# Position bias as a product of two exact factors, and a second expert's first 384 rows beside the attention stage

## The chip, the cores and the metric

The kernel runs on one core of a Trainium2 chip. The metric is device time in microseconds (us). The kernel before took 684.06, 686.87 and 689.18 us in three runs, 686.87 in the median. PE is the matmul engine (PEld its weight loads), DVE, ACT and POOL are the vector, scalar and GpSimd engines, and SP is the engine whose queue issues most of the DMAs. Every engine takes its instructions in the order in which they were emitted.

## What is computed

Eight batches and eight heads of causal attention with a window of 128 and a linear position bias, then a top-1 mixture of eight experts on the 4608 resulting rows of 512:

```python
scores = scale * np.matmul(q, k.transpose(0, 1, 3, 2))      # 8, 8, 576, 576; D = 64
bias = slopes[:, None, None] * (-np.abs(rel))               # rel = query - key
mask = (rel >= 0) & (rel < 128)
attn = softmax(np.where(mask, scores + bias, -1e9))
x = (attn @ v) as rows of 512
expert_idx = argmax(xn @ en.T / tau); gate_w = its softmax value
out[mask_e] = gate_w * (relu(x @ w1[e]) @ w2[e])            # w1 512x1024, w2 1024x512
```

With the inputs used, the experts get 611, 541, 517, 513, 507, 670, 573 and 676 rows; among the first 24 of 36 tiles expert 5 has 479 and expert 7 has 453. The kernel has eight slots with room for 672, 688, 624, 576, 544, 528, 528 and 512 rows (`SLOTS`, L34), and a loop for rows beyond them (L1586) that runs no iteration here.

## The kernel before

**Attention.** The 576 rows of a batch are cut into four tiles of 128 and a rest of 64; the rests of two batches make one "pair" tile. That gives 36 tiles: per two batches two "first" ones (no tile before them in the window), six "full" ones and one pair. A tile is worked in two units of four heads, 72 units in all. A unit is: scores (`score_pe`, L552) into two PSUM banks; for full and pair tiles a merge of the two key blocks by a mask (`merge_dve`), a maximum (`max_dve`), an exponential (`exp_act`), a transpose (`probs_pe`, "flip"), a split into a high and a low half in fp16 (`probs_act`, `probs_dve`), masks on POOL, and the product with v (`values_pe`). `score_pe` first puts the bias into the two banks: an identity matrix (128 rows) is multiplied with a table of the bias in bf16 (L564), which has 512 columns for each bank of a full tile, 256 and 128 in two matmuls for a pair and 256 for a first tile. The q and k products then add to it, as pairs of matmuls on rows 0 to 63 and 64 to 127 of the array. The tables are built at the start (`bias_table`, L268: two "wrap" operations and eight products on DVE for each of two kinds; `first_table`).

**Routing.** Each finished tile is split (`x_act`, `x_pool`), transposed by a DMA (`x_dma`, L738) and gives its logits. Six groups of tiles (`GROUPS`, L39: 8, 8, 8, 6, 4 and 2) are routed together: a chain of small DVE and ACT operations, a matmul for ranks (`ranks`, L790), and scatters of the rows into an array sorted by expert (`put`, L847). The buffers of the split rows (`gx`) are 13 in a ring and come free with the scatters.

**The head.** After the third group (24 tiles) the expert with most rows so far is chosen (`head_ops`, L295). SP reads its number, fetches its weights in 16 pieces of 256 KB (`fetch`, L891) into six staging buffers, ACT and DVE split them (`part_hi`, `part_lo`), its first 384 rows are loaded by a transposing DMA (`head_rows`, L904), and both its matmul layers for them are done in pieces of four matmuls (`head_hidden`, `head_output`) that fill PE between the attention units.

**The expert stage.** `moe` (L1220) then goes through the slots in the order `TURNS` (L35), 0 first and then 1. Slot 0 is the head's expert, from row 384 on; the others take all their rows. `blank_rows` and `rows` (L1258) load a slot's rows, which needs every scatter done; `fetch` and `part` bring and split its weights, by turns into pools `wE`, `wO` and `wT`; `hidden` (L1348) and `output` (L1393) are its matmuls.

**Order.** A planner (`Plan`, L69) writes the order of each engine by hand: every piece of work is a job with an engine, an assumed duration, what it comes after, ring buffers it takes, and a due time. Of the jobs that can start within a slack of the earliest one of an engine it takes those not marked `fill` first, then the one due first. A dependency with `ORDER` fixes only the order of picking. One plan covers attention, routing and head, a second one the expert stage; the whole first plan stands ahead of the second in each queue.

## Time and profile before

| | |
|---|---|
| runs, median (lowest to highest) | 686.87 us (684.06 to 689.18) |
| profiled execution | 687.89 us, of which the span is 686.2 us |
| granted PE clock over the span | 0.974 of full speed |
| busy share PE, PEld, DVE, ACT, POOL | 94, 62, 55, 49, 38% |
| DMA traffic | 109.83 MB, 160 GB/s over the span |

The shares are means over two stages: attention with routing and head up to about 306 us, the experts from 320 us on. A group of instructions is named by its line, engine, operation and tiles (written <- read), and each row gives the start, or the busy time and the mean duration of one. "Idle" is the time in which the engine stood still before an instruction, with what released it.

### The profile page before, as it was taken

What the parts mean: (1) busy time and instruction counts of PE and PEld (TensorE: products, weight loads), DVE (VectorE), ACT (ScalarE), POOL (GpSimd) and SP (SyncE); (2) the same over time, 40 slices, a digit from 0 to 9 for tenths busy, and PEclk for the clock granted to TensorE, in tenths of its full rate; (3) what the DMA queues carried; (4) which work ended last, traced back from release to release, by engine and by line L of the source; (5) the groups of instructions that cost most, each with busy time, mean ns of one, the idle gap of its engine ahead of it and who ended that gap; (6) DMA issues with size and microseconds to landing.
All of it is one profiled execution on the core that took longest, in us unless ns stands there. A gap on an engine that the chain in (4) does not pass through costs nothing. (4 is left out here: it accounts for less than half of the span.)

```text
span 686.2 us, 15721 instructions
## 1 busy us (share of the span) xinstructions
PE 644.3 (94%) x6059; PEld 427.9 (62%) x6059; DVE 380.3 (55%) x985; ACT 332.8 (49%) x777; POOL 257.4 (38%) x427
## 2 busy tenths in 40 slices
PE   8999999998998899883999999999999999999993
PEld 5778767776785667542666476476584764754442
DVE  6888878785896997560336724344244265210250
ACT  5988868885886876410325524333243244210210
POOL 5757578658768635851020110120111112001011
PEclk9999999998999999995999999999999999999998
DMA  9789989896987896247999963924919555001000
GB/s 194 149 146 187 149 229 168 153 194 183 185 171 232 170 217 155 78 116 173 269 234 373 222 260 64 287 99 89 312 48 254 189 101 201 17 16 47 13 31 31
DMA packets 217676, 109.83 MB, mean 160 GB/s; under 512 B 195829, under 2 KB 195829, under 8 KB 217600
## 3 DMA queue, kind: packets, MB, share of 16 engines
q1 hardware_dynamic: 211760, 89.89, 58.1%
q0 software_dynamic: 5840, 18.92, 7.4%
q8 instruction: 48, 0.79, 0.5%
q14 instruction: 28, 0.23, 0.1%
HBM read 61.92 MB, written 28.12 MB: 131 GB/s over the span
## 5 line engine op out<-in xcount | busy, mean ns | idle before, releaser
L1354 PE MATMUL ps<-xT,w1h 128*128 128x272 f16 (+7 forms) x896 | 176.1, 296 | 14.3 <-DMA xT<-xs 13.7
L1354 PE MATMUL ps<-xT,w1l 128*128 128x272 f16 (+7 forms) x448 | 132.7, 296 | 0.0
L1354 PEld LDWEIGHTS <-w1h 128*128 128x128 f16 x896 | 88.4, 99 | 46.1 <-issue 15.2
L365 POOL DMA_INDIRECT out_dram<-y,ids x32 | 35.2, 1099 | 206.0 <-DVE y L1412 107.0
L1362 DVE SCALAR_TENSOR_TENSOR hl<-ps,hh 128x272 f16<-128x272 f32 (+7 forms) x112 | 51.6, 474 | 107.3 <-ACT hh L1364 101.0
L1364 ACT ACTIVATE hh<-ps 128x272 f16<-128x272 f32 (+7 forms) x112 | 45.7, 424 | 115.5 <-PE ps L1354 114.5
L1398 PE MATMUL ps<-w2h,hh 128*128 128x512 f16 (+1 forms) x264 | 98.4, 373 | 0.0
L1398 PE MATMUL ps<-w2l,hh 128*128 128x512 f16 (+1 forms) x264 | 98.4, 373 | 0.0
L1398 PE MATMUL ps<-w2h,hl 128*128 128x512 f16 (+1 forms) x264 | 98.4, 373 | 0.0
L609 ACT ACTIVATE pe<-sc,nm 128x128 f32<-128x128 f32 x288 | 84.6, 378 | 10.9 <-DVE nm L602 8.6
L1398 PEld LDWEIGHTS <-hh 128*128 128x128 f16 x528 | 51.5, 98 | 58.6 <-issue 0.8
L585 PE MATMUL sc<-kh,qh 64*128 64x128 f32 (+2 forms) x768 | 75.5, 343 | 0.5 <-ACT qh L462 0.5
L585 PEld LDWEIGHTS sc<-kh,qh 64*128 64x128 f32 (+1 forms) x768 | 51.4, 182 | 28.3 <-issue 23.9
L462 ACT ACTIVATE pq<-ptp 128x512 f16<-128x512 f32 x72 | 54.2, 753 | 22.0 <-PE ptp L617 14.6
L465 DVE SCALAR_TENSOR_TENSOR pq<-ptp,pq 128x512 f16<-128x512 f32 x72 | 52.8, 733 | 21.0 <-ACT pq L462 18.0
L602 DVE TENSOR_REDUCE nm<-sc 128x2 f32<-128x256 f32 x144 | 55.9, 410 | 4.1 <-PE sc L585 3.6
L617 PE MATMUL ptp<-ident,pe 128*128 128x128 f32 x288 | 48.4, 287 | 10.4 <-ACT pe L609 3.5
L734 POOL TENSOR_TENSOR gx<-xf,gx 128x512 f16<-128x512 f32 x36 | 42.5, 1181 | 30.7 <-DVE gx L723 22.2
L1329 DVE SCALAR_TENSOR_TENSOR w2l<-ws,w2h 128x1024 f16<-128x1024 f32 x28 | 33.9, 1223 | 35.6 <-ACT w2h L1331 33.3
L1354 PEld LDWEIGHTS <-w1l 128*128 128x128 f16 x448 | 44.3, 99 | 15.0
L1329 DVE SCALAR_TENSOR_TENSOR w1l<-ws,w1h 128x1024 f16<-128x1024 f32 x28 | 33.4, 1223 | 35.0 <-ACT w1h L1331 34.9
L1331 ACT ACTIVATE w2h<-ws 128x1024 f16<-128x1024 f32 x28 | 29.1, 1054 | 42.5 <-DMA ws<-moe_w_dram 40.3
(227 smaller groups left out, 1187.5 us busy)
## 6 DMA issues: line engine op xcount, KB each, us to landing
ws<-moe_w_dram SPq DMA_DIRECT2D x56, 512.0 KB
ldk<-k_dram SPq DMA_DIRECT2D x32, 256.0 KB
ldq<-q_dram SPq DMA_DIRECT2D x32, 256.0 KB
ldv<-v_dram SPq DMA_DIRECT2D x32, 256.0 KB
stg<-moe_w_dram SPq DMA_DIRECT2D x16, 256.0 KB
xs<-zrow SPq DMA_DIRECT2D x3, 1092.2 KB
xs<-zrow SPq DMA_DIRECT2D x1, 1413.5 KB
xs<-zrow SPq DMA_DIRECT2D x1, 1285.0 KB
```

What stands on the lines that cost most here:

```text
L462: nc.scalar.activation(hi, ps, AF.Copy, scale=scale)
L465: nc.vector.scalar_tensor_tensor(lo, ps, scale, hi, op0=ALU.mult, op1=ALU.subtract)
L585: nc.tensor.matmul(sc[T, hf, j][o, l, w], qT[T]["h"][rows, hp, o], at["h"][rows, hp, kc], start=False, stop=True, skip_group_check=True,)
L602: nc.vector.tensor_reduce(nm_t[T, hf, j], sc[T, hf, j][:, :, 0:P], axis=AX.X, op=ALU.min)
L609: nc.scalar.activation(pr_t[T, hf][:, 2 * l + j, :], ps[:, l, 0:P], AF.Exp, bias=nm[:, l : l + 1], scale=-1.0)
L617: nc.tensor.transpose(pt[:, i, :], pe[:, i, :], ident)
L734: nc.gpsimd.tensor_tensor(xx[:, DM : 2 * DM], xf_t[T], xx[:, 0:DM], op=ALU.subtract)
L1329: nc.vector.scalar_tensor_tensor(lo_, x, SW, hi, op0=ALU.mult, op1=ALU.subtract)
L1354: nc.tensor.matmul(ps[:, :w], a[:, kt, fs], xx[:, b + kt, c0 : c0 + w], start=(n == 0), stop=(n == len(jobs) - 1))
L1362: nc.vector.scalar_tensor_tensor(hl[:, ft, c0 : c0 + w], ps[:, :w], 0.0, hi, op0=ALU.max, op1=ALU.subtract)
L1364: nc.scalar.activation(hi, ps[:, :w], AF.Relu)
L1398: nc.tensor.matmul(ps, x[:, ft, a * P : (a + 1) * P], w[:, ft, c], start=(n == 0), stop=(n == len(jobs) - 1))
```

## The change

Bias: the bias of query c and key column t is slope x (c + 128 - t) for the tile before and slope x (c - t) for the tile's own keys, that is two products: a column factor (c, 1) and a row factor (slope, slope x (128 - t)). The two factors stand in two rows, padded with zeros to 64, once at partition 0 and once at partition 64; for full and pair tiles one matmul of 64 rows for each of the two banks takes the place of the identity matmuls of 128 rows. The tables for "full" and "pair" go, and `bias_factors` builds the factors.

Second expert: after the third group the expert with the second most rows is chosen too (`second_ops`). Its weights are fetched once the last tile's loads are issued, into 11 `gx` buffers and five staging buffers, and split into the buffers of k, q and v loads and of the transposed k, which are moved to a pool of their own (`rot`) that stays for the expert stage and takes the place of `wO`. Its first 384 rows go through both layers in pieces marked `fill`, behind the head's. Slot 1 then starts at its row 384 with weights that are there. The planner's durations for scores fall, and on DVE and ACT a late, urgent job that can start within 400 ns goes ahead of a fill job.

```diff
+HB = HEAD
+IN_STG = [7, 8, 9, 14, 15]
+GAP = {"DVE": 400, "ACT": 400}
+URGENT = 190000
...
+                if f and e in GAP:
+                    soon = [(t_, j["name"]) for t_, j in lst if not j["fill"] and j["due"] >= URGENT and t_ <= t0 + GAP[e]]
+                    if soon:
+                        t, n = min(soon)
...
+    def bias_factors():
+
+        col = const.tile([P, 2, P], F32, tag="wrap", name="wrap_cols")
+        nc.gpsimd.memset(bcol, 0.0)
+        nc.gpsimd.memset(brow, 0.0)
+        nc.gpsimd.iota(col, pattern=[[-P, 2], [-1, P]], base=P, channel_multiplier=0, allow_small_or_imprecise_dtypes=True)
+        for j in range(2):
+            two, one = slice(64 * j, 64 * j + 2), slice(64 * j, 64 * j + 1)
+            nc.gpsimd.memset(bcol[two], 1.0)
+            nc.gpsimd.iota(bcol[one, 0, :], pattern=[[1, P]], base=0, channel_multiplier=0, allow_small_or_imprecise_dtypes=True)
...
+            for hf in range(2):
+                for l in range(2):
+                    x, sl = brow[:, hf, l], slopes[4 * hf + 2 * l + j]
+                    nc.vector.tensor_scalar(x[two], col[two], sl, None, op0=ALU.mult)
+                    nc.vector.memset(x[one], sl)
...
+            ("DVE", 90, lambda: V.tensor_scalar(k1("r1"), k1("n1"), float(HB), None, op0=ALU.min)),
+            ("DVE", 90, lambda: V.tensor_copy(k1("r1i", I32), k1("r1"))),
+            ("SP", 1500, lambda: head_box["second"]()),
...
-                tab = tabs[kind][:, 4 * hf + j : 4 * hf + j + 3 : 2, :]
-                if kind == "full":
-                    biases = [(ps.rearrange("p l (a c) -> p l a c", a=2), tab.unsqueeze(2).to_broadcast([P, 2, 2, P]))]
-                elif kind == "pair":
-                    biases = [(ps[:, :, 0:P], tab), (ps[:, :, P : P + REM], tab[:, :, 0:REM])]
+                rows = slice(64 * j, 64 * j + 64)
+                if kind == "first":
+                    o, a_, b_ = ps[:, :, 0:P], identb, tabs[kind][:, 4 * hf + j : 4 * hf + j + 3 : 2, :]
                 else:
-                    biases = [(ps[:, :, 0:P], tab)]
-                for n, (o, b_) in enumerate(biases):
-                    nc.tensor.matmul(o, identb, b_, start=(n == 0), stop=False, skip_group_check=True)
+                    w = P + REM if kind == "pair" else 2 * P
+                    o, a_ = ps[:, :, 0:w], bcol[rows, int(kind == "pair"), :]
+                    b_ = brow[rows, hf].rearrange("p l a c -> p l (a c)")[:, :, 0:w]
+                nc.tensor.matmul(o, a_, b_, start=True, stop=False, skip_group_check=True)
...
+        def second_start():
+            sd["e"] = nc.sync.value_load(sel_["se"][0:1, 0:1], min_val=0, max_val=E - 1)
+            sd["r"] = nc.sync.value_load(sel_["r1i"][0:1, 0:1], min_val=0, max_val=HB)
...
+        def second_rows():
+            sd["x"] = xa.tile([P, 2 * KT, HEAD], F16, tag="x_head", name="x_second")
...
-                    f"score{u}", "PE", 660 if first else 1000 if pair else 1300, lambda a=a: score_pe(*a),
+                    f"score{u}", "PE", 660 if first else 850 if pair else 1100, lambda a=a: score_pe(*a),
...
+                f"fetch2_{i}", "SP", 800, lambda i=i: second_fetch(i),
+                after=[second] + ldz + [(f"fetch{x}", ORDER) for x in range(NP)] + [(f"xhi{TL - 2 if i < 10 else TL}", ORDER), (f"xdma{TL if i > 9 else TL - 3}", ORDER)] + ([(f"y{a}", ORDER) for a in range(HEAD // P)] if i in IN_STG[3:] else []) + ([(f"fetch2_{i - 1}", ORDER)] if i else []),
+                makes=[("stg" if i in IN_STG else "gx", ("stg2", i))], due=d,
...
+                made = [(f"k{b}h", ("w1b", b, x)) for b in range(2) for x in range(2)]
...
+            J(f"wlo2_{i}", "DVE", 602, lambda i=i: second_lo(i), after=[f"whi2_{i}"], uses=[("stg2", i)], due=d + 5500, fill=True)
+        J(
+            "rows2", "SP", 3000, second_rows, after=[second, f"hid{FT - 1}_2", (f"xdma{TL}", ORDER)] + ldz + seen, due=due("load", 2 * NT),
+        )
...
+                dep = ["rows2", (f"out{HEAD // P - 1}_5", ORDER)] + [f"wlo2_{w0 + i}" for i in range(KT)] if c == 0 else [f"hid2_{ft}_{c - 1}"]
...
+                dep = [f"hlo2_{ft}" for ft in range(FT)] + [f"wlo2_{2 * KT + i}" for i in range(FT)] if c == 0 else [f"out2_{a}_{c - 1}"]
...
         def first_row(s):
-            return HEAD if s == 0 else 0
+            return {0: HEAD, 1: HB}.get(s, 0)
...
-            if p:
+            if p > 1:
```

The functions of the second expert that are left out (`second_fetch`, `second_hi`, `second_lo`, `second_hidden`, `second_hhi`, `second_hlo`, `second_output`, `second_y`, `second_put`) do what those of the head do, with the same instruction shapes.

## Rows read from the trace of the kernel before

**Rows 1.** One row of the page: the mean clock granted to PE, in tenths, in 40 equal slices of the span.

```profile
PEclk9999999998999999995999999999999999999998
```

**Rows 2.** Busy time by stretches of the span (from:to, length, then PE, PEld, DVE, ACT and POOL busy with the count of instructions, granted clock, DMA share, GB/s), first of the attention stage, then around its end.

```profile
20.00:40.00 20.00, 19.99 (x292) 16.00 (x290) 16.58 (x53) 18.29 (x51) 13.63 (x21) 1.00 0.72 141
60.00:80.00 20.00, 20.00 (x299) 15.70 (x297) 15.52 (x51) 16.82 (x47) 12.28 (x20) 1.00 0.94 148
200.00:220.00 20.00, 16.80 (x220) 12.40 (x216) 13.99 (x54) 12.46 (x36) 15.14 (x26) 1.00 0.78 219
280.00:300.00 20.00, 20.00 (x255) 12.52 (x255) 12.72 (x50) 6.89 (x20) 11.70 (x19) 0.96 0.32 66
306.00:320.00 14.00, 0.41 (x2) 0.00 (x0) 3.40 (x21) 0.00 (x0) 5.06 (x10) 0.60 0.68 181
320.00:326.00 6.00, 5.94 (x26) 3.83 (x27) 0.46 (x1) 0.41 (x1) 0.78 (x4) 0.51 0.73 146
```

**Rows 3.** What PE waited for, longest in total first (total, times, longest one).

```profile
PE ps L1354 <- DMA xT<-xs: 13.7, 1, 13.7
...
PE ptp L617 <- issue: 2.9, 1, 2.9
```

**Rows 4.** PE in order of time at the end of the first plan and the start of slot 0 (start, length, line, operation, count, idle before it).

```profile
305.23 0.17 PE L790 MATMUL ptr<-oh,tri 128*128 128x16 bf16 x1
306.03 0.38 PE L952 MATMUL ps_head<-w2h,hl_head 128*128 128x512 f16 x1
320.06 0.64 PE L1354 MATMUL ps<-xT,w1h 128*128 128x288 f16 x2 [13.66 <-DMA xT<-xs]
```

**Rows 5.** The scatters on POOL and the DMA issues of SP that lead from the last attention tile to slot 0, in order of time, and the head's row load.

```profile
279.26 18.78 SPq L738 DMA_TRANSPOSE xT<-gx  x4
296.80 1.23 SPq L738 DMA_TRANSPOSE xT<-gx  x1
301.00 0.99 POOL L847 DMA_INDIRECT xs<-gx,di  x1 [0.99 <-DVE di L834]
311.00 0.97 POOL L847 DMA_INDIRECT xs<-gx,di  x1 [0.28 <-POOL gx L846]
315.48 2.38 SPq L1265 DMA_TRANSPOSE xT<-xs  x1
L907 SPq DMA_TRANSPOSE x_head<-xs x1: 4275/4275/4275, 225.1 to 225.1; - x1
```

**Rows 6.** Scores on PE, in order of time: of a full unit (bias, q and k product, and the next unit's flip), of a first unit (bias, product) and of a pair unit (bias, product).

```profile
25.25 0.59 PE L564 MATMUL sc<-tab_full,identb 128*128 128x512 bf16 x2
25.77 1.13 PE L585 MATMUL sc<-kh,qh 64*128 64x256 f32 x8
26.84 0.66 PE L617 MATMUL ptp<-ident,pe 128*128 128x128 f32 x4
31.13 0.38 PE L564 MATMUL sc<-tab_first,identb 128*128 128x256 bf16 x2
31.44 0.71 PE L585 MATMUL sc<-kh,qh 64*128 64x128 f32 x8
124.73 0.49 PE L564 MATMUL sc<-tab_pair,identb 128*128 128x256 bf16 x4
125.16 0.88 PE L585 MATMUL sc<-kh,qh 64*64 64x192 f32 x16
```

**Rows 7.** The q and k products of full units as one group up to 300 us, shapes kept apart (count, busy us, mean ns of one).

```profile
L585 PE MATMUL sc<-kh,qh 64*128 64x256 f32 x256 | 37.0, 408 | 0.0
```

**Rows 8.** The head's split of its hidden layer on DVE and ACT, as groups (count, busy us, mean ns of one), and its weights' fetches and DVE halves by line (min/median/max ns, first and last start).

```profile
L935 DVE SCALAR_TENSOR_TENSOR hl_head<-ps_head,hh_head 128x384 f16<-128x384 f32 x8 | 4.4, 551 | 2.7 <-ACT hh_head L931 2.6
L931 ACT ACTIVATE hh_head<-ps_head 128x384 f16<-128x384 f32 x8 | 3.9, 492 | 4.6 <-PE ps_head L928 4.5
L893 SPq MOVE stg<-moe_w_dram x16: 13/29/687, 209.1 to 246.3; - x16
L900 DVE SCALAR_TENSOR_TENSOR w1l<-stg,w1h x8: 653/1258/1653, 221.6 to 241.8; 128x512 f16<-128x512 f32 x8
L900 DVE SCALAR_TENSOR_TENSOR w2l<-stg,w2h x8: 673/682/685, 243.6 to 256.2; 128x512 f16<-128x512 f32 x8
```

**Rows 9.** The head's pieces on PE, in order of time: two matmuls of 384 columns with two more between them, then two of 512 columns, one right after the other.

```profile
273.05 0.33 PE L928 MATMUL ps_head<-x_head,w1l 128*128 128x384 f16 x1
...
273.53 0.33 PE L928 MATMUL ps_head<-x_head,w1l 128*128 128x384 f16 x1
...
303.50 0.38 PE L952 MATMUL ps_head<-w2h,hh_head 128*128 128x512 f16 x1
303.72 0.38 PE L952 MATMUL ps_head<-w2l,hh_head 128*128 128x512 f16 x1
```

**Rows 10.** The start: DVE and POOL work for tables, and the first unit's maximum, in order of time.

```profile
8.15 0.76 DVE L602 TENSOR_REDUCE nm<-sc 128x2 f32<-128x256 f32 x2 [2.02 <-PE sc L585]
9.42 1.84 POOL L995 MEMSET tails<- 128x1024 f16 x2
11.77 1.98 DVE L277 TENSOR_SCALAR tab_pair<-wrap_pair 128x128 bf16<-128x128 f32 x8
```

**Rows 11.** The choice of the head on DVE, first and last of its eight operations.

```profile
205.56 0.15 DVE L305 COPY hc<-ptr 128x8 f32<-128x8 f32 x1
207.96 0.14 DVE L312 CAST he<-hf 128x1 int32<-128x1 f32 x1
```

More of the change, by code (lines that the diff above doesn't have):

```diff
@@ new lines, in second_hidden @@
+        def second_hidden(ft, c):
+            if ft == 0 and c == 0:
+                sd["h"] = [hp_.tile([P, FT, HEAD], F16, tag=f"h{n}_head", name=f"h{n}_second") for n in "hl"]
+            if c == 0:
+                sd["ps1", ft] = bank("sc", [P, 512], name=f"ps1_second_{ft}")[:, :HB]
+            w, ps = head_box["w1b"], sd["ps1", ft]
+            jobs = [(a, b, kt) for kt in range(KT) for a, b in ((0, 0), (0, KT), (1, 0))]
+            for n in range(4 * c, 4 * c + 4):
+                a, b, kt = jobs[n]
+                nc.tensor.matmul(
+                    ps, w(a, kt)[:, ft * P : (ft + 1) * P], sd["x"][:, b + kt, :], start=(n == 0), stop=(n == len(jobs) - 1)
+                )
@@ new lines, in second_hhi, with second_hlo, second_output @@
+        def second_hhi(ft):
+            nc.scalar.activation(sd["h"][0][:, ft, :], sd["ps1", ft], AF.Relu)
+        def second_hlo(ft):
+            hh, hl = sd["h"]
+            nc.vector.scalar_tensor_tensor(hl[:, ft, :], sd["ps1", ft], 0.0, hh[:, ft, :], op0=ALU.max, op1=ALU.subtract)
+        def second_output(a, c):
+            if c == 0:
+                sd["ps2", a] = bank("sc", [P, DM], name=f"ps2_second_{a}")
+            w = head_box["w2b"]
+            jobs = [(x, v_, ft) for ft in range(FT) for x, v_ in ((0, 0), (0, 1), (1, 0))]
+            for n in range(4 * c, 4 * c + 4):
+                x, v_, ft = jobs[n]
+                nc.tensor.matmul(
+                    sd["ps2", a], sd["h"][x][:, ft, a * P : (a + 1) * P], w(v_, ft), start=(n == 0), stop=(n == len(jobs) - 1)
+                )
@@ new lines, in attention @@
+        J(
+            "rows2", "SP", 3000, second_rows, after=[second, f"hid{FT - 1}_2", (f"xdma{TL}", ORDER)] + ldz + seen, due=due("load", 2 * NT),
+        )
+        J("info2", "DVE", 400, second_info, after=["rows2", "order11"], due=1e7)
+        for ft in range(FT):
+            w0 = 0 if ft < FT // 2 else KT
+            for c in range(3):
+                dep = ["rows2", (f"out{HEAD // P - 1}_5", ORDER)] + [f"wlo2_{w0 + i}" for i in range(KT)] if c == 0 else [f"hid2_{ft}_{c - 1}"]
+                J(
+                    f"hid2_{ft}_{c}", "PE", 4 * 162, lambda a=(ft, c): second_hidden(*a), after=dep + ([f"hid2_{ft - 1}_2"] if ft and c == 0 else []),
+                    makes=[(RING["sc"], ("ps1b", ft))] if c == 0 else [], uses=[("ps1b", ft)], due=3e7 + 1000 * ft, fill=True,
+                )
+            J(f"hhi2_{ft}", "ACT", 370, lambda ft=ft: second_hhi(ft), after=[f"hid2_{ft}_2"], uses=[("ps1b", ft)], due=0)
+            J(f"hlo2_{ft}", "DVE", 470, lambda ft=ft: second_hlo(ft), after=[f"hhi2_{ft}"], uses=[("ps1b", ft)], due=0)
@@ new lines, in attention @@
+        for a in range(HB // P):
+            for c in range(6):
+                dep = [f"hlo2_{ft}" for ft in range(FT)] + [f"wlo2_{2 * KT + i}" for i in range(FT)] if c == 0 else [f"out2_{a}_{c - 1}"]
+                J(
+                    f"out2_{a}_{c}", "PE", 4 * 216, lambda b=(a, c): second_output(*b), after=dep + ([f"out2_{a - 1}_5"] if a and c == 0 else []),
+                    makes=[(RING["sc"], ("ps2b", a))] if c == 0 else [], uses=[("ps2b", a)], due=4e7 + 1000 * a, fill=True,
+                )
+            J(
+                f"y2_{a}", "ACT" if a % 2 else "DVE", 600, lambda a=a: second_y(a),
+                after=[f"out2_{a}_5", "info2"] + [f"fetch2_{i}" for i in IN_STG], makes=[("stg", ("y2", a))], uses=[("ps2b", a)], due=2e7,
+            )
+            J(f"yput2_{a}", "POOL", 1200, lambda a=a: second_put(a), after=[f"y2_{a}"], uses=[("y2", a)], due=3e7)
@@ L1376, in passes @@
         def passes(h, w):
[L1377 removed]
+            return [(x, w(v_, ft), ft) for ft in range(FT) for x, v_ in ((h[0], 0), (h[0], 1), (h[1], 0))]
         ps2 = {}
@@ L1481, in moe @@
                         f"hid{n}", 12 * (0.407 * w_ + 5.5), lambda a=a: hidden(*a),
-                        [f"rows{s}"] + ([f"wlo1_{s}_{c}" for c in range(4)] if p else []),
+                        [f"rows{s}"] + ([f"wlo1_{s}_{c}" for c in range(4)] if p > 1 else []),
                         makes=[("pt", ("ps1", n))], uses=[("xT", s), ("w", 1, s)], due=t0,
```

234 lines of the change are left out of this document (180 added, 54 removed).

## Prediction

> **What bounds the kernel now.** I read the clock by slices first: PE runs at full clock but for one slice at half, past the middle [rows 1]. The busy times by stretches say where: in 306 to 320 us PE works 0.41 us of 14, and in 320 to 326 it works with a granted clock of 0.51, the lower level of 1.2 GHz [rows 2]. The list of waits names the largest one of PE, 13.7 us once, until slot 0's rows are loaded [rows 3], and the order of time shows both ends: the head's last piece at 306.03 plus 0.38, slot 0's first matmul at 320.06 [rows 4]. It is a chain of latencies: last x transpose issued at 296.80, last scatter at 311.00, row load at 315.48, first matmul 4.6 us later [rows 5]. Outside it PE is the bound: in 20 to 40 and 60 to 80 it is busy 39.99 us of 40; ACT is next with 18.29 of 20, and the DMA share is 0.94 in the later of the two [rows 2]. From 320 us on no wait of PE is among the long ones [rows 3], so what is taken from PE's work there comes off the end.
>
> **The moved matmuls.** Slot 1 had 688 rows in two chunks, now 384 early and 304 late: the hidden layer has the same 2 x 96 matmuls with the same sum of columns, and 3 + 2 row blocks replace five. PE's work thus neither falls nor rises; it moves from the expert stage to before slot 0. It is 96 matmuls at a pitch of 0.48 / 3 = 0.16 us, 15.4 us, and 72 at 0.216 (303.72 less 303.50, with rounding), 15.5 us [rows 9]: 30.9 us. That is more than the gap, so if the operands are ready it closes the gap wholly: **-13.65 us** of idle time, and the slow clock behind it, 320.06 to about 325.8 at half pace, **-2.9 us** [rows 2, 4]. Slot 0 then starts at about 306.4 + 30.9 + waits, near 340, while its rows are there at 320: the chain has some 19 us of slack, so DVE's 16 weight halves, the puts of the second's rows and everything else that stretches the routing is covered by second-expert matmuls up to that point.
>
> **When its operands come.** Its rows: the transposing load stands on SP right behind the last x transpose, whose issue ends at 298.03. The head's same load took 4.28 us to issue [rows 5]; slot 0's began to be used 2.2 us after its issue ended (320.06 less 317.86), so the rows are there at about 304.5, before the head's last piece. Its w1: tile buffers come free with the last scores (282); fetches go out behind the transpose at 279.26 [rows 5]. At the head's own pace, 209.1 to 242.4 for w1 and to 256.9 for all 16 [rows 8], w1 would be split at 313, when the fifth of eight hidden blocks wants it at 314, and w2 at 327, when the output wants it at 323.5. That pace was DVE's while it was nearly full; in 280 to 300 it is busy 12.72 us of 20 and ACT 6.89 [rows 2]. Late operands: 0 to 5 us, I take **+2**, nearer the lower end because both engines have room. Between the layers PE waits for the last block's halves, 0.49 on ACT and 0.55 on DVE [rows 8] with two handoffs: **+1.5**.
>
> **Transfers in front of transposes.** Ten of the 16 fetches (2.6 MB) may go out between the last four x transposes. PE takes its queue in order and stands at a logit until its transpose has landed. The nearest row is 219.80, where PE stood 2.9 us for nothing that the trace shows, while the head's fetches were in flight [rows 3]. Three transposes behind fetches: 0 to 8.7 us, I take **+3**, one such stop, because the last transposes are up to 5 us apart. Fetches 10 to 13 wait for the buffers of tiles 30 to 33, whose scatters begin at 301.00 [rows 5]; behind them on SP stand only the blanking and rows of slot 0, which have the slack above.
>
> **The choice of the second.** Twelve more DVE operations and two reads on SP. The head's eight took 205.56 to 208.10, 0.32 each [rows 11], so 3.8 us more before SP can go on; queued behind it are fetches, loads and transposes. PE is busy only 16.80 of 20 us there [rows 2]. 0 to 3 us, I take **+1**.
>
> **The bias.** A full unit's bias takes 25.25 to 25.77, 0.52 us, for two matmuls of 512 columns (2 x 0.216, and 0.09 until the next weights are in); a first unit's, half the columns, takes 0.31, a pair's 0.43 [rows 6]. That two 64-row matmuls run side by side the trace shows: eight q and k products of 408 ns each [rows 7] take 1.07 us from their start to the flip [rows 6], while at the pitch of 0.216 of a matmul of about this length (0.38, [rows 9]) they would take 1.73. So a full unit falls to about 0.31, as the first unit with the same columns in a row: 48 x 0.21 = 10.1 us; a pair unit from 768 columns in a row to 384: 8 x 0.16 = 1.3 us. Of 11.4 us PE time the first 200 us give most, where PE is full, but the next bounds are near (ACT 91% and DMA 0.94 [rows 2]), and where PE waits for others nothing is gained. Bounds 0 and -11.4; I take **-8**, nearer the upper end since the packed stretches hold most units.
>
> The Trainium skill, TensorEngine Tiling (Array Packing), Key Properties, speaks against a part of it: a change of tiling mode drains the engine. In full units the change only moves from behind the bias to before it; in pair units (64 x 128, then 64 x 64) one is added. No row here shows such a drain by itself; by the rule the pair units' gain would be near nothing and the sum about 1 us higher.
>
> **The start.** On DVE the four wrap operations and the pair table (1.98 us, [rows 10]) go; eight products and eight small memsets come, some 3 us, but ahead of the first unit's maximum (8.15) and behind about 2.6 us of POOL work, of which one memset of 128 x 1024 is half of 1.84 [rows 10]. The first units come up to 2.7 us later, and what the pair table delayed comes earlier. -1 to +3, I take **+1**.
>
> **Sum.** 687.89 (this execution) - 13.65 - 2.9 - 8 + 2 + 1.5 + 3 + 1 + 1 = 671.8. The execution is 1.0 us above the median of the runs; for the median that is **671 us**.
>
> **Rivals.** *The bias pays nothing*: the two matmuls run one after the other, or ACT and DMA set the pace. For it: ACT's 18.29 of 20; against: PE's 39.99 of 40 and the pairs of q and k products. 671 + 8 = 679. *The operands come late*: the matmuls stand where I put them, but PE waits 11 us for them instead of 2, w2 above all, since six of its eight fetches stand behind the last transpose and the scatters. Then 671 + 9 = 680. *Slower, the gap moves*: if the second's pieces stand in PE's queue before the last group's rank matmul (305.23, [rows 4]), the chain from there to slot 0, 14.8 us, begins only when they are done, and its idle time and slow clock stand behind them instead of before. Nothing is won at the end, the waits of 8.5 us remain: 687.89 - 1 + 8.5 - 8 = 687 with the bias's gain, 695 without. It decides from about 19 us of delay of that matmul on. For it: both stand in one fixed order made with assumed durations; against: fill pieces yield to any job that is ready, and these need a load behind the last transpose.
>
> **Chances.** Forecast 0.62 (664 to 678), bias nothing 0.13, late operands 0.14, gap moves 0.06, better than 664 0.05 (at best 661: -11.4 for the bias and no wait but 1.5 and the start). About 1% (680 and 694 us) is what a measurement of this kernel can tell from no change. Faster: 0.62 + 0.05, half of each of the two cases at the border, which spread some us around 679 and 680, less a little for waits that add up: 0.78. Same: the rest of these and most of the moved gap, 0.16. Slower: 0.06, the moved gap without the bias's gain, or several waits at their upper ends. The range reaches from the best case's neighbourhood to late operands at their worst, 660 to 683.
>
> **What would show it.** The bias: between its first matmul and the first q and k product 0.3 us in place of 0.52, and the two bias matmuls starting together; the last scores come some 8 us earlier. The gap: PE's wait for slot 0's rows gone, no slice at half clock, slot 0 starting 12 to 20 us after 320 less what attention gained, at full clock. The waits: idle of PE before second-layer pieces under 3 us. I am wrong if PE stands more than 10 us in all before the second's matmuls, if units keep their spacing (3 us and more) with a shorter bias, or if later expert slots wait for weights.

## The result and the profile after

The changed kernel takes 692.22 us (median of 6 runs, 690.17 to 693.65) against 687.19 of the kernel before: 1.0073 times, 95% interval 1.0049 to 1.0097. I had said 671 us. Its profiled execution took 691.89 us with a span of 689.8.

The clock by slices (as [rows 1]) and busy time by stretches (as [rows 2]):

```profile
PEclk9999999999998999997999999999999999999998
```

```profile
20.00:40.00 20.00, 19.80 (x287) 16.78 (x289) 17.76 (x55) 18.50 (x52) 14.20 (x20) 1.00 0.69 133
280.00:300.00 20.00, 18.50 (x235) 11.34 (x228) 12.22 (x38) 8.98 (x25) 12.88 (x19) 0.91 0.76 199
300.00:320.00 20.00, 8.77 (x81) 4.48 (x79) 12.46 (x40) 5.01 (x14) 11.35 (x17) 0.81 0.51 134
320.00:326.00 6.00, 6.00 (x35) 3.29 (x34) 3.50 (x21) 3.70 (x7) 0.57 (x2) 0.78 0.92 280
360.00:380.00 20.00, 16.24 (x88) 8.76 (x86) 10.84 (x17) 8.30 (x14) 0.97 (x1) 0.91 0.81 209
```

There still is a hole, with a lower clock in it and behind it: PE works 8.77 us of 20 in 300 to 320. And there is a second, small one in 360 to 380, where before was nearly full. Before, in the same stretch:

```profile
360.00:380.00 20.00, 19.33 (x121) 11.62 (x119) 13.01 (x17) 11.93 (x19) 0.00 (x0) 1.00 1.09 351
```

What PE waited for (as [rows 3]):

```profile
PE ptl L813 <- DMA xT<-gx: 14.0, 6, 8.6
...
PE ps L1644 <- DVE hl L1608: 3.8, 1, 3.8
PE ps_second L1117 <- DMA x_second<-xs: 2.6, 1, 2.6
```

The wait for slot 0's rows is gone, as intended. In its place PE waits for the x transpose of the last attention tile, for the second expert's rows, and inside slot 0. PE in order of time (as [rows 4] and [rows 6]): the bias and the product of a full unit, the last two scores (with one matmul of the head's output layer ahead of the last), the last logit, the second's first piece, the last rank matmul, slot 0's hidden and output layer.

```profile
269.20 0.39 PE L633 MATMUL sc<-brow,bcol 64*128 64x512 bf16 x2
269.42 0.39 PE L654 MATMUL sc<-kh,qh 64*128 64x128 f32 x4
...
279.17 0.34 PE L633 MATMUL sc<-brow,bcol 64*128 64x384 bf16 x2
...
290.45 0.38 PE L1021 MATMUL ps_head<-w2l,hh_head 128*128 128x512 f16 x1
290.76 0.34 PE L633 MATMUL sc<-brow,bcol 64*128 64x384 bf16 x2
...
316.87 0.28 PE L813 MATMUL ptl<-enc,xT 128*128 128x16 f16 x4 [8.61 <-DMA xT<-gx]
...
319.87 2.72 PE L1117 MATMUL ps_second<-x_second,w 128*128 128x384 f16 x8 [2.63 <-DMA x_second<-xs]
322.39 0.22 PE L859 MATMUL ptr<-oh,tri 128*128 128x16 bf16 x1
...
353.48 0.42 PE L1600 MATMUL ps<-xT,w1h 128*128 128x288 f16 x2 [0.85 <-DVE y_second L1144]
...
369.17 0.38 PE L1644 MATMUL ps<-w2h,hh 128*128 128x512 f16 x1 [3.76 <-DVE hl L1608]
```

Read from the end: the last logit waits for a transpose whose issue comes at 312.41 instead of 296.80 [rows 5]. POOL and SP, in order of time:

```profile
300.86 0.88 POOL L719 TENSOR_SCALAR_AFFINE_SELECT tails<-pq 64x256 f32<-64x256 f32 x2 [7.69 <-DVE cd L894]
...
304.90 0.97 POOL L916 DMA_INDIRECT xs<-gx,di  x1 [0.28 <-POOL gx L915]
...
310.07 1.12 POOL L916 DMA_INDIRECT xs<-gx,di  x1 [0.28 <-POOL gx L915]
311.22 1.16 POOL L803 TENSOR_TENSOR gx<-xf,gx 128x512 f16<-128x512 f32 x1
```

```profile
312.41 1.23 SPq L807 DMA_TRANSPOSE xT<-gx  x1
313.83 3.95 SPq L1084 DMA_TRANSPOSE x_second<-xs  x1
```

The last unit's mask begins at 300.86, so its rows are late; the lower half of the last x (311.22) then stands on POOL behind the four scatters of the group before. And the unit is late from its score on: 290.76 against 280.64 in before:

```profile
280.64 0.85 PE L564 MATMUL sc<-tab_pair,identb 128*128 128x256 bf16 x4
```

Between the last two scores PE does, beside the flips and the products with v of other units, much of the head's output layer (two of its three products in the 11.8 us from 279, by operand):

```profile
L1021 PE MATMUL ps_head<-w2h,hh_head x9: 378/379/381, 278.6 to 290.2; 128*128 128x512 f16 x9
L1021 PE MATMUL ps_head<-w2l,hh_head x9: 379/379/379, 278.9 to 290.5; 128*128 128x512 f16 x9
```

In before no output piece stands ahead of the last score (the first one starts at 283.55); here eight do, of four matmuls each, six of them between the last two scores. The planner wrote it so: a score takes two of the four banks of the ring `sc`, an output block one, and a bank is handed on in turn. With the shorter durations that the change gives scores (1100 and 850 ns), block 0 is planned just ahead of the last score but one, and the last score's second tile then falls to block 0's bank and cannot be planned until the block is finished; block 1 fills the time.

Slot 0's own wait is ACT's order. ACT, then SP:

```profile
365.22 1.06 ACT L1577 ACTIVATE w2h<-ws 128x1024 f16<-128x1024 f32 x1 [17.05 <-DMA ws<-moe_w_dram]
366.44 1.06 ACT L1577 ACTIVATE w2h<-ws 128x1024 f16<-128x1024 f32 x1 [0.16 <-DMA ws<-moe_w_dram]
367.40 2.50 ACT L1610 ACTIVATE hh<-ps 128x288 f16<-128x288 f32 x8
```

```profile
348.35 6.43 SPq L1550 DMA_DIRECT2D ws<-moe_w_dram  x4
354.97 1.38 SPq L1552 DMA_DIRECT2D ws<-moe_w_dram  x2
```

ACT stands 17.05 us at slot 4's weight halves, whose loads SP issues from 348.35 on; the eight halves of slot 0's hidden layer stand behind and then run without a wait, in 2.50 us.

### The profile page after: what moved, and what is told of

Read it like the earlier page. It is cut to its first block, busy times and chain, and to the rows that moved or that the text cites. A ratio compares the mean times of both kernels' runs of the same rounds, so it can differ in the third digit from the quotient of the medians.

```text
span 689.8 us, 15768 instructions
## 1 busy us (share of the span) xinstructions
PE 634.5 (92%) x6043; PEld 425.4 (62%) x6043; DVE 384.6 (56%) x1015; ACT 334.1 (48%) x785; POOL 257.8 (37%) x440
## 4 chain that ended last, share of the span: by engine, by line
PE 71%; DMA 8%; DVE 7%; POOL 5%; ACT 4%; issue 3%; SPq 1%; POOLq 0%; ACTq 0%
PE ps L1644 22%; PE ps L1600 21%; PE sc L654 5%; PE av L754 5%; DMA xT<-gx 4%; PE ptp L686 4%; PE ps_second L1117 2%; PE ptk L543 2%; PE sc L633 2%; PE ps_t L1634 2%; DMA ws<-moe_w_dram 2%; PE ps_second L1135 2%; POOL xs L916 1%; PE ptq L543 1%; ACT pq L532 1%
## 5 line engine op out<-in xcount | busy, mean ns | idle before, releaser
L1608 DVE SCALAR_TENSOR_TENSOR hl<-ps,hh 128x272 f16<-128x272 f32 (+5 forms) x104 | 47.1, 469 | 97.6 <-ACT hh L1610 90.0
L1600 PE MATMUL ps<-xT,w1h 128*128 128x272 f16 (+4 forms) x448 | 81.2, 284 | 0.8 <-DVE y_second L1144 0.8
L1600 PE MATMUL ps<-xT,w 128*128 128x288 f16 (+4 forms) x576 | 78.9, 299 | 0.0
L1600 PEld LDWEIGHTS <-w 128*128 128x128 f16 x576 | 56.4, 98 | 22.4
L1600 PE MATMUL ps<-xT,w1l 128*128 128x272 f16 (+4 forms) x224 | 63.6, 284 | 0.0
L1644 PE MATMUL ps<-w2h,hh 128*128 128x512 f16 x152 | 58.3, 384 | 3.8 <-DVE hl L1608 3.8
L1644 PE MATMUL ps<-w2l,hh 128*128 128x512 f16 x152 | 58.4, 384 | 0.0
L1644 PE MATMUL ps<-w2h,hl 128*128 128x512 f16 x152 | 58.2, 383 | 0.0
L1600 PEld LDWEIGHTS <-w1h 128*128 128x128 f16 x448 | 43.8, 98 | 12.1 <-DVE y_second L1144 1.3
L1644 PE MATMUL ps<-w,hh 128*128 128x512 f16 (+1 forms) x176 | 48.1, 360 | 0.0
```

The costliest lines, as they stand in the source:

```text
L1600: nc.tensor.matmul(ps[:, :cw], w(a, kt)[:, fs], xx[:, b + kt, c0 : c0 + cw], start=(n == 0), stop=(n == len(jobs) - 1))
L1608: nc.vector.scalar_tensor_tensor(hl[:, ft, c0 : c0 + w], ps[:, :w], 0.0, hi, op0=ALU.max, op1=ALU.subtract)
L1644: nc.tensor.matmul(ps, x[:, ft, a * P : (a + 1) * P], w[:, c], start=(n == 0), stop=(n == len(jobs) - 1))
```

## The experiments

The runs were timed in six series, each with the kernel before beside it: that took 686.0 to 687.2 us in three of them and 680.4 to 681.0 in the others. So each run is given as its ratio to before in its own series; 1% is some 6.9 us, and the expected times in us were written for a before of 686 to 687. One kernel timed in two series gave 0.9947 and 0.9984 (`out_after`, `out_after_2`), another 0.9840 and 0.9839 (`old_durations`, `old_durations_2`): between series, less than 0.4% tells nothing. "Old durations" are 1300 and 1000 ns for a full and a pair unit's score in the planner, "new" are the change's 1100 and 850. They change only the order that the planner writes. Scores are counted from 1 to 72.

**The bias alone, then with an earlier start.** `bias_alone` is the kernel before with the new bias:

```diff
-                for n, (o, b_) in enumerate(biases):
-                    nc.tensor.matmul(o, identb, b_, start=(n == 0), stop=False, skip_group_check=True)
+                nc.tensor.matmul(o, a_, b_, start=True, stop=False, skip_group_check=True)
...
+        J("factors", "DVE", 3500, bias_factors, due=due("score", 1))
```

> The kernel before with only the bias changed to the product of two factors; the planner keeps its old durations for scores (1300 and 1000 ns), so the fixed order of the work stays that of before. Theory (the bias is cheaper on PE but attention is paced by other things, and the factors come late at the start): full units show 0.23 us from bias to first q and k product where before showed 0.52, the score of the third unit starts near 13.6 us where before had 10.59, and the last score stays within 2 us of 280.6; time 685 to 690 us. Rival (my prediction's term of -8 us): the last score comes near 273 us and the time is 677 to 681 us.

Measured 0.9971 (0.9950 to 0.9991), 684.64 us. The fourth score of before, then the fourth and the last one here:

```profile
13.22 0.59 PE L564 MATMUL sc<-tab_full,identb 128*128 128x512 bf16 x2
```

```profile
17.23 0.39 PE L579 MATMUL sc<-brow,bcol 64*128 64x512 bf16 x2
...
276.27 0.34 PE L579 MATMUL sc<-brow,bcol 64*128 64x384 bf16 x2
```

Against 13.22 and 280.64 in before that is 4.0 us late, then 4.4 early. Between them 8.4 us are gained, my rival's figure; half of it makes up for the start. Neither expectation holds whole: the last score is earlier than the theory allows, the time longer than the rival's. `bias_start` moves the factors:

```diff
         bias_rel("full")
+        bias_cols()
         bias_table("full")
         first_table()
+        bias_rows()
...
-        J("factors", "DVE", 3500, bias_factors, due=due("score", 1))
+        J("factors", "POOL", 1600, bias_factors, due=due("v", 0))
```

> The kernel before with the bias as a product (as in the run of the bias alone, old durations, same order) and the factors made earlier at the start. It tells the bias's gain from the start's cost. In the run of the bias alone the third and fourth units came some 3 to 4 us late and the last unit 4.3 us early, so units 4 to 72 gained 8.3 us. Theory (both are real and both go through to the end): third unit's score at 11 to 11.5 us, last score 7 to 8 us before that of before, ratio to before 0.989 to 0.993, that is 5 to 7.5 us less. Rival (the 8 us are only regained lateness, since the first units were late and the rest is paced by other engines): ratio 0.996 to 0.999, as the bias alone.

Measured 0.9923 (0.9894 to 0.9952), 5.3 us less than before. The third and the last score:

```profile
12.04 0.39 PE L587 MATMUL sc<-brow,bcol 64*128 64x512 bf16 x2
...
275.36 0.50 PE L587 MATMUL sc<-brow,bcol 64*128 64x384 bf16 x2
```

The ratio is the theory's and not the rival's. The scores fall short of it: the third is 0.5 us later than it said, and the last one comes 5.3 us before that of before and not 7 to 8 (the profiled execution, 686.46 us, was the slowest of six). The two ratios lie 0.0048 apart, 3.3 us, which I take as the start's cost; their intervals just touch, and they are of two series.

**The second expert alone, and the late score.** `second_alone` is the changed kernel with the old bias and the old durations.

```diff
-                    f"score{u}", "PE", 660 if first else 850 if pair else 1100, lambda a=a: score_pe(*a),
+                    f"score{u}", "PE", 660 if first else 1000 if pair else 1300, lambda a=a: score_pe(*a),
```

> The changed kernel with the old bias (matmul of the identity with the table, old durations in the planner), so only the second expert's early rows are new. In the order that the planner then writes, the last score stands ahead of the head's output pieces again. Theory (the late last score of the changed kernel came from the head's output taking a bank of the score ring first, set off by the new durations): the last score starts at 279 to 283 us, PE's waits at the last logit and at the second's rows fall from 11.2 us to under 4, slot 0 starts near 345, time 677 to 684 us (the wait of 3.8 us in slot 0 stays). Rival (the second expert's work moves the gap whatever the order): 688 us or more.

Measured 0.9919 (0.9888 to 0.9950), 680.61 us. Last score, slot 0's start and slot 0's output:

```profile
284.00 0.49 PE L618 MATMUL sc<-tab_pair,identb 128*128 128x256 bf16 x4
...
343.26 0.42 PE L1584 MATMUL ps<-xT,w1h 128*128 128x288 f16 x2 [0.85 <-DVE y_second L1129]
...
358.95 0.38 PE L1628 MATMUL ps<-w2h,hh 128*128 128x512 f16 x1 [3.76 <-DVE hl L1592]
```

The gap is closed; the same 3.76 us stand in slot 0. `out_after` is the changed kernel with one dependence more:

```diff
-                dep = [f"hlo{ft}" for ft in range(FT)] + [f"wlo{2 * KT + i}" for i in range(FT)] if c == 0 else [f"out{a}_{c - 1}"]
+                dep = [f"hlo{ft}" for ft in range(FT)] + [f"wlo{2 * KT + i}" for i in range(FT)] + [("score71", ORDER)] if c == 0 else [f"out{a}_{c - 1}"]
```

> The changed kernel, with the order of one thing set: the head's output pieces may stand in PE's queue only after the last score. Theory (bank of the score ring): the last score starts at 280 to 284 us instead of 290.76, the last x transpose is issued by 301 instead of 312.41, PE's waits of 8.6 us at the last logit and 2.6 us at the second's rows fall below 4 together, slow clock around them goes; slot 0 starts at 341 to 346 instead of 353.48 and the time is 678 to 684 us. Rival (transposes are late behind the second's fetches, or POOL's puts stand in the way whatever the score does): the waits stay above 8 us, time 688 to 692 us.

Measured 0.9947 (0.9922 to 0.9971), 681.80 us: by the ratios 1.25% below the change (0.9% with the 0.9984 of `out_after_2`, the same kernel). Last score, last logit, second's first piece, slot 0:

```profile
279.74 0.34 PE L633 MATMUL sc<-brow,bcol 64*128 64x384 bf16 x2
...
303.34 0.25 PE L813 MATMUL ptl<-enc,xT 128*128 128x16 f16 x4
...
308.01 0.48 PE L1117 MATMUL ps_second<-x_second,w 128*128 128x384 f16 x2
...
341.50 0.42 PE L1600 MATMUL ps<-xT,w1h 128*128 128x288 f16 x2 [0.84 <-DVE y_second L1144]
```

The score comes 11.0 us earlier, slot 0 12.0, and neither the last logit nor the second's rows are waited for. One dependence undoes the hole, so the last score's place was its cause. `old_durations` is the whole change with the old durations (the line shown for `second_alone`).

> The changed kernel, whole, but the planner is given the old durations of the scores (1300 and 1000 ns), with which it writes the order of the run with the second expert alone. Theory (the new durations set off the late last score; bias and second expert are both worth something and add up): last score at 278 to 281 us, PE's waits at the last logit under 3 us, 677 to 680 us, that is the second expert alone (680.6) less the 2 us of the bias alone. Rival 1 (without the new durations the bias is worth nothing once the gap is closed): 680 to 682 us. Rival 2 (the order was not it): 688 us or more.

Measured 0.9840 (0.9802 to 0.9878), 675 us of 686, last score at 269.64. Both rivals are out, and both figures are better than the theory's; the gain is more than the sum of the two parts (0.0029 + 0.0081), about as far as the intervals allow. Against the change this one line is worth 2.3%, 16 us. `out_after_start`, the changed kernel with the dependence and the earlier factors:

> As the run before it, and the bias factors made earlier: POOL writes the column factors right after the distances and before the first table, one product on DVE fills both rows of a head (8 products in place of 8 products and 8 memsets), all ahead of the first maximum. Theory (the start costs 3 us and they go through to the end): the third unit's score starts at 10.4 to 11.2 us instead of 13.62 and the time is 2 to 3 us below the run before it. Rival (attention is paced later by other things and swallows the start): the time is within 1 us of the run before it.

Measured 0.9859 (0.9820 to 0.9898), the third score at 11.37: 3.6 us less than `out_after` by the medians and 0.9% by the ratios, more than the 2 to 3 us expected, with intervals that almost touch.

**Slot 0's wait.** `weights_first`:

```diff
+                        first3 = p == 2 and (w_, c) < (2, 2)
+                        if first3:
+                            d = -15000 + 1000 * (4 * w_ + c)
...
-                        J(f"get{w_}_{s}_{c}", "SP", 1456, lambda a=a: fetch(*a), makes=[("ws", key)], due=d, after=before(f"blank{s}") + ([(f"get{w_}_{s}_{c-1}", ORDER)] if c else []))
+                        J(f"get{w_}_{s}_{c}", "SP", 1456, lambda a=a: fetch(*a), makes=[("ws", key)], due=d, early=handed["order"] if first3 else 0.0, after=([] if first3 else before(f"blank{s}")) + ([(f"get{w_}_{s}_{c-1}", ORDER)] if c else []))
```

> The changed kernel, with only this moved: the first six weight loads of the third expert in turn (slot 4) stand on SP before the blanking and the rows of slot 1 instead of behind them and behind slot 4's blanking. Theory (ACT, which takes its queue in order, stood at w2's halves of slot 4 waiting for these loads, with eight of slot 0's halves queued behind): the loads are issued before 345 us, PE's wait of 3.8 us for slot 0's lower half and the slow clock after it are gone, 686.5 to 689 us against 692.2. Rival (another late operand takes its place, such as slot 1's rows, which now stand behind 3 MB of weights): 691 us or more, with a new wait of PE between 350 and 380 us.

Measured 1.0080 (1.0052 to 1.0107): no gain that can be told. (687.78 us lies in the theory's range only because before took 680.97 here.) The loads are out by 340.1 and slot 0 waits no more, but PE waits again one slot later, where the rival had not put it: three times in slot 1's output, 3.0 us in all, after ACT stood 7.70 and 2.23 us at weight halves whose loads were not there:

```profile
390.45 0.39 PE L1649 MATMUL ps<-w,hl 128*128 128x512 f16 x1 [0.72 <-DVE hl L1613]
393.03 0.61 PE L1649 MATMUL ps<-w,hh 128*128 128x512 f16 x2 [1.54 <-ACT hh L1615]
394.36 0.39 PE L1649 MATMUL ps<-w,hl 128*128 128x512 f16 x1 [0.72 <-DVE hl L1613]
```

`late_halves` has the old durations and the earlier factors, leaves the loads and moves ACT's weight halves, by a longer planned time from load to half in every slot:

```diff
-                            after=[f"get{w_}_{s}_{c}"] + ([(f"whi{w_}_{s}_{c-1}", ORDER)] if c else []), makes=[(ring, ("w", w_, s))] if c == 0 else [], due=d + 3000, fill=True,
+                            after=[(f"get{w_}_{s}_{c}", 12000)] + ([(f"whi{w_}_{s}_{c-1}", ORDER)] if c else []), makes=[(ring, ("w", w_, s))] if c == 0 else [], due=d + 3000, fill=True,
```

> Changed kernel with old durations and the earlier factors; slot 4's loads stand where the change put them, but the planner counts 12 us more from a weight load's issue to its first half on ACT, so that in ACT's queue the hidden layer's halves of the slot that runs stand before the next slot's weight halves. Theory (ACT's order, not the loads' time, made PE wait): no wait of PE over 1.5 us behind the last pieces of the second expert, against 3.3 to 3.8 before; ratio to before 0.973 to 0.977, as good as or better than with the earlier loads (0.9781). Rival (the loads' time itself is the limit): a wait of 2 us or more stays and the ratio is 0.978 to 0.982.

Measured 0.9757 (0.9728 to 0.9786); what is left of slot 0's wait:

```profile
353.38 0.39 PE L1652 MATMUL ps<-w2h,hl 128*128 128x512 f16 x1 [0.46 <-DVE hl L1616]
```

From slot 0's first matmul to the end of the span it takes 331.4 us, against 336.3 in the change, 335.8 in `old_durations` (which has the same planner durations) and 335.9 in `weights_first`. So it was ACT's order, worth some 5 us. `weights_and_late_halves` has 8000 in place of 12000, and the earlier loads too.

> As the run before it with 8 us in place of 12, and slot 4's first six loads earlier as well. Theory (with ACT's order mended the loads' place is worth little more): within 0.3% of the run before it, no wait over 1.5 us. Rival (both are needed): 0.4% or more below it, with waits left in the run before it.

Measured 0.9742 (0.9713 to 0.9771), no difference that can be told, and 330.7 us from slot 0 on: the loads' place is worth little. The same repairs without the later halves, under old and under new durations:

> The run before it (old durations), with the bias factors made earlier at the start and slot 4's weights loaded earlier. Theory (each cost is separate and goes through to the end): 678.5 less 3 to 3.5 for the start less 3.8 for the wait in slot 0, that is 670 to 673 us, no wait of PE over 2.5 us after the first. Rival (attention swallows the start's gain, as transfers or the order of the queues set its pace): 674 to 677 us.

> The changed kernel with new durations and all three repairs: head's output pieces behind the last score, bias factors earlier, slot 4's weights earlier. Theory: 678.2 less the remaining waits in slot 0 (1.2 us) and a little slow clock, 675 to 678 us; it stays above the run with the old durations, because in the order that the new durations give the scores from the 65th on come 5 us later (score 65 at 248.9 us in the order with the new durations, 245.7 with the old). Rival (both orders are worth the same once the last score is free): equal within 1.5 us to the run with the old durations.

Measured 0.9781 (0.9764 to 0.9799), 671 us of 686, as its theory said, and 0.9911 (0.9882 to 0.9940), 680 us of 686, more than its theory's 675 to 678 and further still from its rival. `all_three` waits 3.7 us in slot 1, where the other waits 1.8, and it stays 1.3% above: the order of the new durations costs more than the late score.

**What else the new durations cost: not settled.** Two suspects of that order were undone alone, each on top of `out_after`: head's hidden pieces taken early (12 instead of 4 ahead of the 65th score), and tile 32's loads behind 12 instead of 9 of the head's fetches on SP. `hidden_paced`:

```diff
+PACE = [(4, 64), (9, 65), (13, 66), (18, 69), (21, 71)]
...
+                dep = dep + [(f"score{x}", ORDER) for n, x in PACE if 3 * ft + c >= n][-1:]
```

> The changed kernel with its new durations, head's output pieces behind the last score, and the 24 pieces of the head's hidden layer spread as in the order with the old durations: at most 4 ahead of the 65th score, 9 ahead of the 66th, 13, 18 and 21 ahead of the 67th, 70th and 72nd (the new durations put 12, 16, 20 and 24 there). Theory (in the order that the new durations give, the head's pieces push the last scores, and with them the routing, back): within 0.3% of the run with the old durations, 0.982 to 0.987 of before. Rival (the free last score was all there was to it; the difference to the old durations came from the two being timed on two chips): all three runs of this call within 0.4% of each other.

> The run with only the head's output pieces set behind the last score, once more, beside the run with the old durations on one chip. Theory (hidden pieces too): 0.8% to 1.3% slower than the old durations. Rival (two chips): within 0.4% of it.

> The run with the old durations of the scores once more, on the same chip as the two others. 0.981 to 0.987 of before if the first timing of it holds on this chip; 0.988 to 0.993 if that came from the chip.

In one series: 0.9997 (0.9980 to 1.0014), 0.9984 (0.9969 to 0.9999) and 0.9839 (0.9799 to 0.9880). So the difference between the two orders is real, 1.45% with the last score free, and spreading the hidden pieces does not remove it. In `hidden_paced` PE stands, with fewer pieces to fill the time, at a logit whose transpose is late:

```profile
241.73 0.26 PE L814 MATMUL ptl<-enc,xT 128*128 128x16 f16 x4 [4.35 <-DMA xT<-gx]
...
246.30 0.39 PE L634 MATMUL sc<-brow,bcol 64*128 64x512 bf16 x2
```

`loads_first`:

```diff
-            J(f"fetch{i}", "SP", 800, lambda i=i: fetch(i), after=[started] + then("score", min(at, 71)), makes=[("stg", ("stg", i))], due=d)
+            J(f"fetch{i}", "SP", 800, lambda i=i: fetch(i), after=[started] + then("score", min(at, 71)) + ([("load_q32", ORDER)] if i >= 9 else []), makes=[("stg", ("stg", i))], due=d)
```

> The changed kernel with new durations and the head's output pieces behind the last score, and in addition SP's order set so that the key and query loads of tile 32 come ahead of the head's tenth weight fetch, as in the order with the old durations; with the new durations twelve fetches stood ahead of them. Theory (what still cost 1% in the order of the new durations is this: the 65th score came 8 to 10 us after the key load's issue in every order, and the load was issued 30 to 31 us after the first fetch with the new durations, 23 to 27 with the old): the load's issue falls to 23 to 28 us after the first fetch, from score 64 to score 65 it takes 9 to 13 us in place of 16 to 17, ratio to before 0.983 to 0.990. Rival (the loads are not it either): ratio 0.994 to 1.000, as the two runs that only free the last score.

Measured 0.9956 (0.9936 to 0.9976), from the 64th to the 65th score 18.3 us. The time is the rival's, but the load came late all the same, behind an x transpose that SP was issuing until 237.83:

```profile
237.88 0.58 SPq L464 DMA_DIRECT2D ldk<-k_dram  x1
```

That is 28.1 us after the first fetch, at the edge of the 23 to 28 that the theory asked for (28.2 in `new_all`, 29.0 to 31.4 in the other runs with the new durations, 21.7 to 26.7 with the old). In every trace the 65th score comes 7.6 to 11.7 us after this load's issue. So the run shows that the number of fetches ahead is not the cause; whether the late load is, it does not show. The two scores lie 16 to 20 us apart in every run with the new durations and 8 to 13 with the old, before among them (11.2); what makes it so stays open.

`new_all` is `loads_first` with the three other repairs, `best_again` is `weights_and_late_halves` once more.

> The run before it with the three other repairs too: bias factors earlier, slot 4's first loads earlier, weight halves later in ACT's order. Theory (with the causes undone, the new durations are worth the same as the old): within 0.5% of the best so far (0.9742), run beside it here. Rival (something else in the order of the new durations costs): 0.982 or more.

> The best kernel so far (old durations, factors earlier, slot 4's loads earlier, halves later), beside the two others on one chip: 0.972 to 0.977 of before.

0.9786 (0.9758 to 0.9814) and 0.9738 (0.9704 to 0.9771) in one series: with everything repaired about 0.5% lies between the two orders, with intervals that overlap. The 64th and the 65th score still lie 16.7 us apart in `new_all`; its last score comes 4.5 us after that of `best_again`, its slot 0 only 2.0. The best version is the whole change with the old durations, the earlier factors and loads, and the later halves: 2.6% faster than before, 663.32 us where before took 680.57.

## Why the prediction was wrong, point by point

**Where the 20 us went.** The sum gave 671.8, the execution took 691.89. Slot 0 was to start at 337.8 (320.06 - 13.66 + 30.9 + 1.5 + 2 + 3 + 1 + 1 - 8.0) and started at 353.48: 15.7 us too late. From there to the end it took 338.4 us; the sum had 334.0 (687.89 - 320.06 - 2.9 - 30.9). By the same terms the last score was to come at 275 to 278 (280.64 - 8 + 1 + 1, and up to the 3) and came at 290.76: 13 to 16 us late, so nearly all of the 15.7 us lie ahead of it.

**The gap: the step that failed.** That "the rows are there at about 304.5, before the head's last piece" rested on a last transpose issued where it stood, at 296.80. I moved matmuls in the order but left the rest of the order alone, although the change gives the planner new durations, and every job of the plan is placed by them: that effect I put at nothing, without a reason. It measures 2.3%, 16 us (1.0073 against 0.9840 of `old_durations`). "Fill pieces yield to any job that is ready" was true and beside the point: the last score could not be planned, because a fill piece had its bank. The rival of the moved gap named the right kind of thing (0.06), but for the rank matmul behind the second's pieces; that one came at 322.39 behind two of them (eight matmuls), while the chain was already late by its head, the score. The score's place is worth 11.0 us at the score and 6 to 9 of the 16 us (10.4 by the medians, 692.22 less 681.80; 8.6 by the ratios; 6.1 with the ratio of `out_after_2`). The rest, 7 to 10 us (1.45% in the series that has both orders), arises at least in part ahead of the last score too (275.55 in `out_after_2`, 271.46 in `old_durations_2`), and its cause is open.

**What followed: sized well, in part by luck.** From the last score to slot 0 the sum needed 60 to 63 us and 62.7 were measured, but otherwise made up: 11.2 us of wait for transpose and rows against some 7 us of output layer done in advance. Without the late score it is 61.8 (`out_after`) and 59.3 (`second_alone`). "-13.65" and "-2.9" were right: the wait for slot 0's rows is gone, `second_alone` and `old_durations` have no other in its place, and in `out_after` the granted clock is 1.00 from 300 to 330. "Late operands +2" holds for the weights: no piece waits for one (one in `out_after`, 0.8 us). "+3" for transposes behind fetches fits too: without the late score PE waits 1.8 to 4.4 us for them in all, 0.9 in before. "+1.5" between the layers is not seen; the output layer follows at 336.93 without a wait. No run separates the "+1" of the choice.

**The bias: right for full units, for a wrong reason; -8 at the upper end.** From bias to product it is 0.22 us. But the last score shows what stands ahead of it now: the matmul of 512 columns takes 0.31 (290.45 to 290.76) where another 128-row matmul follows after 0.22 [rows 9]; at 384 columns it is 0.26 in after, and 0.16 in before, where the bias had 128 rows. So some 0.10 us stand at each of these steps from 128-row to 64-row matmuls, and a full unit takes 0.32, about the 0.31 that I costed. The 0.09 that I had put down to "until the next weights are in" is this step; it only moved from behind the bias to before it. From a pair unit's bias to its product it is 0.26 (279.17 to 279.43) where before took 0.43, and with the 0.10 ahead the gain is 0.07, not 0.16. The Trainium skill, TensorEngine Tiling (Array Packing), Key Properties, says that a change of tiling mode drains the engine; by it the pair's gain would be near nothing. The trace agrees: some 0.10 us at each change, and 0.7 us less gain over the eight pair units. In time the term is 5.3 us by `bias_start`, whose fourth score (14.67) still is 1.5 us late, and 8.4 us between the fourth and the last score of `bias_alone`, where part may be lateness made up: inside the bounds 0 and -11.4, with -8 at the upper end of what was measured.

**The start: the term was mis-sized.** "+1, bounds -1 to +3" measured some 3 us: 3.0 by the third score of after, 3.5 by its fourth (16.74), 3.3 by the two ratios. I let what the pair table had delayed come earlier and pay for it; the first maximum waits for the sixteen DVE operations (6.62 to 11.23 in the trace of after; it starts at 11.40, in before at 8.15), and the flip and the third score behind them: 13.62 in place of 10.59.

**Slot 0: a step that was missing.** "From 320 us on no wait of PE is among the long ones [rows 3], so what is taken from PE's work there comes off the end": it had none there while the second in turn loaded its weights during slot 0 (issued from 321.32 on). Now those are there, the third's loads go out at 348.35 behind the rows of two slots, and ACT stands at them in order: 3.76 us, and a clock of 0.91 in 360 to 380. That accounts for most of the 4.4 us from slot 0 on, 338.4 against 334.0. I had named it as what would make me wrong ("later expert slots wait for weights") and given it no price. `late_halves` takes some 5 us of it away.

With the planner's durations left alone the change comes out at 0.984, 676 us on the scale of the 686.87, within the range that I gave, although the start and slot 0 cost some 2 and 4 us more than the sum had for them; with the start and ACT's order mended too at 0.976, 670 (`late_halves`).

## What to carry to other kernels

Where a planner orders the work from assumed durations, a new duration is a change of its own: list which jobs trade places on every engine before costing the rest, and look first at the jobs at the head of the chain that ends last. A fill piece has low priority for its engine but holds its bank or buffer like any other; give such pieces an order against the last job of the chain. Before a load is moved forward because an engine stands at its result, see what stands behind that instruction in the engine's queue: here moving the instruction back cut the wait from 3.3 and 4.1 us (`old_durations` and its repeat) down to 0.46, while moving the load alone left 3.0 us of it, one slot on.

## What the runs showed that I had not expected

One kernel, before, had medians of 686.0 to 687.2 us in three series and 680.4 to 681.0 in three others, 0.9% apart, as much as the change itself moved the time; only runs of one series can be compared in microseconds. Of the slower ones two were timed on chips 3 and 6, the faster ones on chip 10 (twice) and chip 2; that the chip makes the difference fits this, but no chip was timed at both levels. A step from 128-row to 64-row matmuls shows as some 0.10 us each time. And an x transpose, 1.23 us to issue at 296.80 [rows 5], took 3.59 and 4.28 us in `loads_first` at 234 and 244 us, behind a load that followed the head's fetches. The fetches alone do not make it so: in before one took 1.23 us at 244.88, right behind four fetches, and one 3.10 at 250.11, behind three tile loads. What does was not tested.
